# Row-tiled projections and two-bank vector work in a mixed attention and mixture-of-experts kernel

## The chip, the cores and the metric

One core of one Trainium2 chip. The metric is device microseconds (us) for one execution. The kernel before takes 1044.51 us (median of 3 runs, 1044.15 to 1045.33).

Engine names as the profile has them: PE is the matrix engine (PEld its weight loads), DVE the vector engine, ACT the scalar engine, POOL the general engine. PSUM is the memory that the matmuls write (`P` and `ps` in the profile); the kernel uses it as eight banks of 512 fp32 columns. A "512-column matmul" moves 512 columns. The "granted clock" is the share of PE's full clock that the profile records as granted: 1.00 is full speed, "half clock" is 0.5. A "ring" is a set of buffers that are handed out in turn.

## The reference, cut to what matters

```python
def phi(x):                                   # q and k: 8 batches, 8 heads, 576 rows, 64 dims
    proj = einsum('bhsd,df->bhsf', x, w_phi)  # contraction over 64, 128 features
    proj = proj - max(abs(proj), axis=-1)
    return concatenate([exp(proj), exp(-proj)], axis=-1)
kv  = einsum('bhsf,bhsd->bhfd', phi(k), v)
out = einsum('bhsf,bhfd->bhsd', phi(q), kv) / (einsum('bhsf,bhf->bhs', phi(q), z) + 1e-6)
x   = out as (4608, 512)                      # input of the mixture of experts
P   = exp(x @ w_gate - max); 8 rounds of row and column normalisation
y   = sum over 8 experts e of P[:, e] * (relu(x @ w1[e]) @ w2[e])
```

The contraction of the projections runs over 64 only, half of the 128 rows that the profile gives for these matmuls (`128*128`). That is what the change is aimed at.

## The kernel before: the parts that matter

Attention works on 32 pairs of heads (8 batches, 4 pairs). All operations of attention and of the first expert (expert 0, used as filler work for PE) are put into a list, with costs; a Python list scheduler then decides the order of every engine. A string gives the priority of the steps.

```python
order = (   # a: keys, q: queries, r: rest rows, b: kv and numerators, c: transposes, g: gate,
            # u/d: expert 0 up/down.  Cut; 188 steps in all
    "aqraqabbcqabqacbqrbcaqbacuqaqbacqruabgqccucbudbduaqabdqadgrcbucqucabqcauqdua" ...)

ring(ps, [128, 512], FP32, "P1", 8)          # eight PSUM buffers of one bank each
ring(a_t, [128, 2, 4, 128], BF16, f"q{x}", 2)   # rings of two for the tiles of a pair

def scores(x, n):                            # keys (x=1) and query maxima (x=0); n is 1
    for c0 in range(0, 4, 2 * n):
        pp = new(f"P{n}")
        for c in range(2 * n):               # wphi2f: 128 x 256, block-diagonal copies of w_phi
            pe(256, ... mm(pp()[:, 256*c:256*c+256], qkT(x, c0 + c, 1), wphi2f, True, True) ...)
        maxes(512 * n, ...)                  # DVE, one bank
        if x == 1:
            for y, sg in ((0, 1.0), (1, -1.0)):
                exp(512 * n, ...)            # ACT, one bank

def queries():
    mq = scores(0, 1)
    for p0 in range(0, 2, 1):
        pt = new("P1")
        pe(512, ... mm(pt()[:, 0:512], wphi2[:, p0, :], qkT(0, 0, 4), True, True) ...)
        for y, sg in ((0, 1.0), (1, -1.0)):
            exp(512, ...)                    # ACT, one bank

def up(w1, g, hT, fcs, n, r=(), w=()):       # expert 0: four contraction steps of 512 columns
    for f0 in fcs[::n]:
        ph = new(f"P{n}")
        for i in range(n):
            for dc in range(NP):
                pe(512, ... mm(ph()[...], w1()[:, dc, ...], xT[:, dc, ...], dc == 0, dc == NP - 1) ...)
        act(512 * n, ... Relu from ph to hT ...)
```

Two heads lie in the two halves of the partitions. The block-diagonal weight, padded with zeros, projects both at once with the whole array: half of the multiplications are by zero.

## Time and profile before

| stage | span (us) | what runs |
|---|---|---|
| attention mixed with expert 0 | 0 to 219 | all engines; 78 to 209 is its full part |
| leftover expert 0, routing beneath it | 219 to 263 | PE back to back |
| experts 1 to 7 | 263 to 1043 | PE back to back |

The head of the profile's page: busy time of each engine, its share of the span, and its instructions.

```profile
span 1043.5 us, 24529 instructions
PE 1020.4 (98%) x9512; PEld 842.1 (81%) x9512; DVE 823.9 (79%) x1626; ACT 711.1 (68%) x1570; POOL 461.5 (44%) x532
PEclk9999999999999999999999999999999999999999
```

The table of windows for the start and the full part of attention. Columns: window, length, busy us of each engine (number of instructions), then PE's granted clock, DMA share, GB/s.

```profile
core 0: us, PE busy (x) PEld busy (x) DVE busy (x) ACT busy (x) POOL busy (x), PEclk, DMA share, GB/s
0.00:26.00 26.00, 17.36 (x147) 12.63 (x147) 17.09 (x36) 18.26 (x45) 9.59 (x25) 1.00 0.94 250
26.00:52.00 26.00, 21.91 (x252) 14.39 (x252) 24.56 (x60) 24.23 (x63) 21.75 (x40) 1.00 1.01 150
78.00:209.00 131.00, 129.49 (x1426) 83.78 (x1425) 118.38 (x295) 123.00 (x315) 82.91 (x166) 1.00 0.81 133
```

In the full part all three engines look nearly level: PE 99%, ACT 94%, DVE 90%.

The groups of instructions before 220 us (PE) and in 78 to 209 us (DVE, ACT): line, engine, operation, names, shapes and count; then busy us, mean ns of one; then idle time before it and what ended it. One fence for each engine.

```profile
L407 PE MATMUL P<-wphi,qkT 128*128 128x256 bf16 x256 | 39.3, 277 | 1.5 <-DVE wphi L760 0.8 <-DVE xb_r L631 0.3 <-DVE m L399 0.2
L407 PE MATMUL P<-qkT,wphi 128*128 128x512 bf16 x64 | 21.6, 387 | 1.4 <-DVE m_r L399 0.9 <-DVE m L399 0.5
```

```profile
L399 DVE TENSOR_REDUCE m<-P 128x4 f32<-128x512 f32 x81 | 52.6, 681 | 0.5 <-ACT k L403 0.4
```

```profile
L403 ACT ACTIVATE q<-P 128x512 bf16<-128x512 f32 x82 | 46.2, 630 | 3.5 <-PE P L606 2.2 <-PE P L407 1.2
L403 ACT ACTIVATE k<-P 128x512 bf16<-128x512 f32 x84 | 44.3, 629 | 1.6 <-PE P L407 1.5
```

The two PE lines are the work that the change tiles: 256 and 64 matmuls.

Three stretches of PE's timeline (start, duration, engine, line, operation): a group of four projections, the last gate group, and the first matmuls of expert 1.

```profile
178.23 0.60 PE L407 MATMUL P<-wphi,qkT 128*128 128x256 bf16 x4
178.66 0.55 PE L407 MATMUL P<-wgate,xT 128*128 128x8 bf16 x16
...
218.91 0.95 PE L407 MATMUL P<-wgate,xT 128*128 128x8 bf16 x32
...
263.21 0.60 PE L1019 MATMUL P<-xT,w 128*128 128x256 bf16 x4
```

The marked durations overlap (the group of four is marked 0.60 us long, and the next group starts 0.43 us after it), so starts are what to read. The group of four holds PE from 178.23 to 178.66, 0.109 us for 256 columns. The last gate group (the matmuls `x @ w_gate` of the last rows) marks the end of attention.

### The profile page before, as it was taken

What the parts mean: (1) busy time and instruction counts of PE and PEld (TensorE: products, weight loads), DVE (VectorE), ACT (ScalarE), POOL (GpSimd) and SP (SyncE); (2) the same over time, 40 slices, a digit from 0 to 9 for tenths busy, and PEclk for the clock granted to TensorE, in tenths of its full rate; (3) what the DMA queues carried; (4) which work ended last, traced back from release to release, by engine and by line L of the source; (5) the groups of instructions that cost most, each with busy time, mean ns of one, the idle gap of its engine ahead of it and who ended that gap; (6) DMA issues with size and microseconds to landing.
All of it is one profiled execution on the core that took longest, in us unless ns stands there. A gap on an engine that the chain in (4) does not pass through costs nothing.

```text
span 1043.5 us, 24529 instructions
## 1 busy us (share of the span) xinstructions
PE 1020.4 (98%) x9512; PEld 842.1 (81%) x9512; DVE 823.9 (79%) x1626; ACT 711.1 (68%) x1570; POOL 461.5 (44%) x532
## 2 busy tenths in 40 slices
PE   6899999999999999999999999999999999999998
PEld 4566666654788888888888888888888888888886
DVE  6999899998777787778877787778777877787775
ACT  7999999944976666666666666565666666666663
POOL 3876757500233344344444444444444443333442
PEclk9999999999999999999999999999999999999999
DMA  9997987734411152113311441134111611114333
GB/s 250 150 196 132 150 127 136 122 122 120 93 41 41 52 105 60 51 42 82 81 41 42 87 87 51 42 69 95 41 42 50 125 51 42 41 43 131 122 122 122
DMA packets 105237, 93.94 MB, mean 90 GB/s; under 512 B 45344, under 2 KB 80288, under 8 KB 105120
## 3 DMA queue, kind: packets, MB, share of 16 engines
q1 hardware_dynamic: 71840, 68.45, 23.6%
q0 software_dynamic: 33120, 23.86, 16.4%
q8 instruction: 74, 1.21, 0.5%
q14 instruction: 43, 0.35, 0.1%
q10 hardware_dynamic: 160, 0.07, 0.0%
HBM read 94.98 MB, written 14.16 MB: 105 GB/s over the span
## 4 chain that ended last, share of the span: by engine, by line
PE 89%; ACT 5%; DVE 3%; DMA 1%; issue 1%; SPq 0%; POOL 0%; DVEq 0%; ACTq 0%
PE P L1019 70%; PE P L407 16%; ACT acc L1181 2%; DVE m L399 1%; PE P L606 1%; ACT k L403 1%; DMA acc<-in_q_dram 1%; DMA wgate_f<-in_moe_w_gate_dram 1%; ACT V L1171 1%; ACT U L1047 1%; PE P L645 1%; DVE xb L626 0%; ACT q L403 0%; DVE P L618 0%; PE P L484 0%
## 5 line engine op out<-in xcount | busy, mean ns | idle before, releaser
L1174 POOL TENSOR_TENSOR acc<-acc,V 128x512 f32<-128x512 f32 x248 | 316.4, 1283 | 440.4 <-ACT V L1171 437.2
L1051 DVE CUSTOM_DVE_ANT_0 hT<-P,U 128x512 bf16<-128x512 f32 x378 | 255.0, 687 | 107.9 <-ACT U L1047 59.7
L1047 ACT COPY U<-P 128x512 f32<-128x512 f32 x378 | 217.8, 590 | 137.4 <-PE P L1019 130.8
L1171 ACT ACTIVATE V<-P,P 128x256 f32<-128x256 f32 x496 | 206.3, 477 | 123.4 <-PE P L1019 121.6
L1159 DVE SCALAR_TENSOR_TENSOR acc<-P,P,acc 128x256 f32<-128x256 f32 x372 | 160.1, 478 | 73.4 <-PE P L1019 71.7
L1019 PEld LDWEIGHTS <-w 128*128 128x128 bf16 x2016 | 197.3, 98 | 23.7 <-issue 0.6
L1019 PEld LDWEIGHTS <-S 128*128 128x128 bf16 x1984 | 194.1, 98 | 23.2 <-issue 0.6
L1019 PEld LDWEIGHTS <-T 128*128 128x128 bf16 x1512 | 147.9, 98 | 19.1 <-issue 2.0
L1019 PEld LDWEIGHTS <-hT 128*128 128x128 bf16 x1488 | 145.4, 98 | 18.3 <-DVE hT L1051 1.1
L1019 PE MATMUL P<-X,w 128*128 128x256 bf16 x1008 | 154.7, 273 | 0.4 <-ACT U L1047 0.4
L1019 PE MATMUL P<-xT,w 128*128 128x256 bf16 x1008 | 152.0, 273 | 0.0
L1019 PE MATMUL P<-X,T 128*128 128x256 bf16 x1008 | 148.6, 273 | 1.3 <-ACT U L1047 1.2
L1019 PE MATMUL P<-w,hT 128*128 128x256 bf16 x992 | 142.6, 273 | 0.6 <-DVE hT L1051 0.6
L1019 PE MATMUL P<-T,S 128*128 128x256 bf16 x1056 | 136.3, 273 | 0.4 <-ACT V L1171 0.4
L1019 PE MATMUL P<-w,S 128*128 128x256 bf16 x928 | 126.6, 273 | 0.0
L532 POOL TENSOR_TENSOR v<-v_m,em 128x512 bf16<-128x512 f32 x64 | 66.8, 1043 | 70.6 <-ACT em L403 57.5
L399 DVE TENSOR_REDUCE m<-P 128x4 f32<-128x512 f32 x128 | 82.7, 681 | 1.7 <-PE P L407 1.2
L1056 ACT ACTIVATE hT<-P 128x512 bf16<-128x512 f32 x126 | 74.6, 607 | 12.9 <-PE P L1019 12.4
L407 PE MATMUL P<-w,hT 128*128 128x512 bf16 x320 | 80.2, 379 | 0.3
L927 DVE TENSOR_TENSOR S<-hT 128x1024 bf16<-128x1024 bf16 x124 | 80.1, 683 | 0.0
L407 PE MATMUL P<-xT,w 128*128 128x512 bf16 x288 | 76.2, 379 | 1.2 <-ACT kr L403 0.5
L1019 PE MATMUL P<-xT,T 128*128 128x256 bf16 x504 | 76.3, 273 | 0.0
(94 smaller groups left out, 1091.7 us busy)
## 6 DMA issues: line engine op xcount, KB each, us to landing
X<-xd SPq DMA_DIRECT2D x126, 256.0 KB, 2.6
w<-in_moe_w_dram POOLq DMA_DIRECT2D x14, 1024.0 KB, 10.4
v_m<-in_v_dram SPq DMA_DIRECT2D x15, 512.0 KB, 5.1
out_dram<-acc SPq DMA_DIRECT2D x14, 512.0 KB, 3.2
xd<-S SPq DMA_DIRECT2D x18, 256.0 KB, 2.0
qk<-in_k_dram POOLq DMA_DIRECT2D x12, 256.0 KB, 5.5
qk<-in_q_dram POOLq DMA_DIRECT2D x12, 256.0 KB, 6.4
w<-in_moe_w_dram POOLq DMA_DIRECT2D x8, 256.0 KB, 7.5
```

The lines of the kernel that those rows point to most:

```text
L399: dve(el, lambda: nc.vector.tensor_reduce(out=dst(), in_=src(), axis=AX.X, op=ALU.max, apply_absolute_value=True), r, w)
L407: nc.tensor.matmul(out_, lhsT=lhsT, rhs=rhs, start=start, stop=stop)
L532: pool(512, lambda y=y, em=em: nc.gpsimd.tensor_tensor(out=s["v"][y]()[:, :, 0:D], in0=t["v"]()[:, h0:h0 + 2].rearrange("p a (b c) -> p (a ...
L927: lambda: f.tensor_tensor(out=out_(), in0=x(), in1=y(), op=op), r, w, **kw)
L1019: pe(256, lambda i=i, k=k, z=z: nc.tensor.matmul(bank()[:, 256 * i:256 * i + 256], lhsT=lhs(k, i), rhs=rhs(k), start=first and z, stop=k = ...
L1047: act(512, lambda: nc.scalar.copy(out=u[fp][n]().rearrange("p a b -> p (a b)"), in_=x[fp]()), [x[fp]], [u[fp][n]])
L1051: dve(500, lambda: nc.vector._custom_dve(ADD_SAT, out=out_(fp, i, j), in0=bank[fp]().rearrange("p (a b) -> p a b", a=2), in1=u[fp][n](), s ...
L1056: act(512, lambda: nc.scalar.activation(out=out_(fp, i, j), in_=x[fp]().rearrange("p (a b) -> p a b", a=2), func=ACT.Relu, bias=0.0, scale ...
L1159: dve(330, lambda n=n, ts=ts: nc.vector.scalar_tensor_tensor(out=acc[g][:, ts, 256 * j:256 * j + 256], in0=bank()[:, 256 * n:256 * n + 256 ...
L1171: act(390, lambda n=n: nc.scalar.activation(out=u()[:, n, :], in_=bank()[:, 256 * n:256 * n + 256], func=ACT.Copy, bias=0.0, scale=P[:, 4 ...
L1174: pool(670, lambda: nc.gpsimd.tensor_tensor(out=acc[g][:, 2 * i:2 * i + 2, 256 * j:256 * j + 256], in0=acc[g][:, 2 * i:2 * i + 2, 256 * j: ...
L1181: act(512, lambda ts=ts: nc.scalar.activation(out=acc[g][:, ts, :], in_=acc[g][:, ts, :], func=ACT.Copy, bias=0.0, scale=P[:, 4 * g + ts, ...
```

## The change

Its intent: (1) each zero-padded projection becomes two matmuls of 64 rows, meant to run on the upper and the lower half of the array at the same time, each writing its own PSUM bank; (2) query maxima, query exps and numerators read two neighbouring banks in one instruction, so ACT and DVE issue fewer; (3) more buffers for the tiles of a pair, placed inside the second weight tiles, which are idle during attention; (4) finer steps in the order string (query maxima and query features apart, kv and numerators apart). PSUM becomes one tile whose banks are handed out one or two at a time.

```diff
-        def scores(x, n):
-            for c0 in range(0, 4, 2 * n):
-                pp = new(f"P{n}")
-                for c in range(2 * n):
-                    pe(256, lambda c=c, c0=c0, pp=pp: mm(
-                        pp()[:, 256 * c:256 * c + 256], qkT(x, c0 + c, 1), wphi2f,
+    def mm2(banks, stat, mov, n):
+        for c in range(n):
+            for x in range(2):
+                rows = slice(64 * x, 64 * x + 64)
+                w = 512 // n
+                nc.tensor.matmul(banks[x]()[:, w * c:w * c + w],
+                                 lhsT=stat(c)[rows], rhs=mov(c)[rows], start=True, stop=True)
+    def pe2(cols, two_, stat, mov, n, r, takes=()):
+        plan.op("PE", n * max(cols / 2400.0 + 0.0025, 0.06) + 0.08, 0.32,
+                lambda: mm2(two_[1], stat, mov, n), r, two_[0], takes)
+        def scores(x):
+            merged = (1, 0)[x]                 # query maxima take two neighbouring banks
+            pp = two(merged)
+            pe2(128, pp, lambda c: qkT(x, c, 1), lambda c: wphi, 4, ...)
+        def queries():
+            pt = two(1)
+            pe2(512, pt, lambda c: wphi, lambda c: qkT(0, 0, 4), 1, ...)
@@ cut: numerators in one two-bank tile; rings @@
-    ring(ps, [128, 512], FP32, "P1", 8)
+    R["P1"], R["P2"] = Banks(ps, banks, 1), Banks(ps, banks, 2)
-        ring(a_t, [128, 2, 4, 128], BF16, f"q{x}", 2)
+        ring(a_t, [128, 2, 4, 128], BF16, f"q{x}", 2, 1)     # 1 more, inside the weight tile
@@ cut: the order string, now with p (query features) and n (numerators) as steps of their own @@
```

A "group" below is one call of `mm2`: eight tiled matmuls of 128 columns, or two of 512. There are 104 of them.

## The prediction

> **What bounds it now.** The windows view splits the span in three. (1) Attention mixed with expert 0, 0–219 us: in 78–209 us PE is marked busy 129.5 of 131 us, ACT 123.0, DVE 118.4; in 0–78 us PE 63.6, ACT 67.5, DVE 66.9 of 78. (2) Leftover expert-0 matmuls, 219–263 us, back to back on PE; routing (P written at 257.6) hides under them. (3) Experts 1–7, 263–1043 us, matmuls at a pitch of 0.109 us per 256 columns. The chain of waits is 89% PE. The change touches mainly stage 1[...]. With PE pitches from the timeline (0.216 us per 512 columns, 0.03 per 65) I sum about 189 us of PE work before the last gate, which ends at 219.7. ACT, 190.5 of 209 us, looks tightest.
>
> **What changes, with durations from the trace.**
> - ACT: 128 query exps of 512 become 64 of 1024; 32 kr exps of 256 become 16 of 512: 80 instructions fewer. 512 columns have a pitch of 0.49 us, about 0.06 above streaming. About −5 us.
> - DVE: five instructions fewer per pair (a maximum, a multiply, a reciprocal, two xb), 160 in all, each with a fixed part of about 0.07 us (a 512-wide maximum repeats every 0.60 us). About −11 us.
> - PE: projections become pairs of 64-row matmuls. [...] With perfect concurrency 189 becomes about 169 us. The changed instruction order has 172 mode switches; at an estimated 0.05–0.1 us each (part of the 0.17 us that a short matmul lasts beyond its pitch) 9–17 us come back. Net −3 to −11 us.
> - Deeper pair rings and finer steps let ACT and DVE wait less; of ACT's 19 idle us before 209, about 8 are the DMA-fed start and stay.
> - Expert 1's weights load after attention. A megabyte lands in 10.4 us (DMA issues), routing takes 38 us: hidden.
> - Banks are picked most recently freed first. In the expert stage the PE work between a bank's last write and its reuse falls from a median of 4.8 us (minimum 2.0) to 2.7 (mostly at least 1.3), by the instruction order. An eviction takes 0.6–0.7 us, so I expect 0–4 us of small PE waits.
>
> **On the critical path.** Attention's end moves with the tightest engine: ACT, about 185 us of work plus 14 idle, then the tail. I expect the last gate at about 209 instead of 220 us (−10), everything after it shifted, +1 for bank reuse.
>
> **Predicted: 1035 us**, 8 in 10 within 1026–1044. Faster by over 2%: 5%; within 2%: 92%; slower: 3%. More than 2% would need attention to end before 199 us, with some 185 us of ACT work in it.
>
> **What would show each step.** 64 query exps of 1024 at about 1.05 us; DVE busy before the last gate about 10 us lower; paired matmuls starting within nanoseconds of one another, and a gap around each group; last gate near 209 us; expert 1 starting near 253 us, its stage (780 us) unchanged within 4; no wait for expert 1's weights.
>
> **What would make it wrong.** Row tiles that do not overlap, or switches of 0.15 us and more: PE becomes tightest and the gain vanishes. An order that front-loads attention and then starves PE. Bank reuse that stalls every one of the 63 groups: +5 to +10 us. Upwards: packing that removes nearly all ACT idle.

The sum was 1044.5 us, 10 less by an earlier last gate and 1 more for bank reuse, given as 1035. In PE's term the 20 us of streaming saved (189 to 169) stand on an assumption, "with perfect concurrency", and the 9 to 17 us that come back on the estimate from the 0.17 us. The item on ACT and that on DVE do not say how streaming was told from the fixed part. Back-to-back starts before 220 us (medians) do: ACT's are 0.263 and 0.477 us apart for 256 and 512 columns in the kernel before, and 0.905 for 1024 in the changed one, so one instruction for two saves 0.049 us; DVE's maxima are 0.598 us apart for 512 (before) and 1.131 for 1024 (after), so it saves 0.065 us.

## The result, and the profile after

The changed kernel takes 1044.51 us (median of 4 runs, 1044.21 to 1044.92); the kernel before took 1044.92 us (1044.15 to 1046.4) in the same rounds. The ratio is 0.9994, with a 95% interval of 0.998 to 1.0008: the same time. It was predicted at 1035 us, and 1044.51 is outside the range of 1026 to 1044. A ratio here is the mean time of one kernel's fast runs over that of the other's of the same rounds, so it is not quite the ratio of the medians quoted beside it.

The same views of the changed kernel. First the head of the page:

```profile
span 1042.4 us, 24890 instructions
PE 1014.3 (97%) x9819; PEld 832.6 (80%) x9864; DVE 817.4 (78%) x1466; ACT 709.1 (68%) x1490; POOL 463.3 (44%) x532
PEclk9899999999999999999999999999999999999999
```

DVE has 160 instructions fewer and ACT 80, as foreseen. PE shows 9819 matmuls but 9864 weight loads: 45 matmul records are missing from this trace, so its idle time can't be taken from matmul starts without care.

The windows:

```profile
0.00:26.00 26.00, 18.41 (x155) 14.08 (x157) 15.53 (x27) 17.85 (x40) 13.17 (x32) 0.93 0.98 255
26.00:52.00 26.00, 20.25 (x299) 15.01 (x298) 24.02 (x42) 22.83 (x49) 17.88 (x35) 0.80 0.96 142
78.00:209.00 131.00, 126.76 (x1644) 73.71 (x1670) 113.61 (x193) 120.83 (x267) 80.77 (x161) 1.00 0.74 119
```

DVE is 4.8 us less busy and ACT 2.2 us in the full part. PE's 126.76 lacks the missing records. PE's granted clock is 0.93 and 0.80 in the first two windows, where it was 1.00. The clock records show two stretches at half clock, at 21.7 us for 3.4 us and at 38.7 us for 10.2 us. Sixteen 65-column matmuls in a row are marked 1.09 us long in the second of them, at 46.38 us, and 0.68 us before it, at 36.48 us. In the 3.4 us before each stretch PE streamed for 1.1 and 1.2 us, and its longest marked wait was 1.40 and 0.94 us. In the profiled execution of the untiled kernel of the same order (e1, below) there was no such stretch in the first 50 us. What sets the half clock off was not shown.

The groups:

```profile
L500 PE MATMUL ps<-wphi,qkT 64*128 64x128 bf16 x512 | 26.2, 230 | 4.4 <-DVE m L476 1.0 <-DVE xb L719 1.0 <-DVE wx L476 0.7
L500 PE MATMUL ps<-qkT,wphi 64*128 64x512 bf16 x64 | 13.2, 412 | 1.7 <-DVE m L476 1.1
```

```profile
L476 DVE TENSOR_REDUCE m<-ps 128x4 f32<-128x512 f32 x28 | 18.9, 682 | 1.6 <-PE ps L500 1.4
L476 DVE TENSOR_REDUCE m<-ps 128x8 f32<-128x1024 f32 x15 | 18.3, 1218 | 2.3 <-PE ps L500 2.3
```

```profile
L480 ACT ACTIVATE k<-ps 128x512 bf16<-128x512 f32 x56 | 29.5, 610 | 1.0 <-PE ps L500 0.8
L480 ACT ACTIVATE q<-ps 128x1024 bf16<-128x1024 f32 x28 | 27.5, 1030 | 1.5 <-PE ps L500 1.1
```

(Buffers that lie inside the weight tile appear as `wx` in lines of their own, so the counts here are not whole.) Busy time of the tiled projections fell from 39.3 to 26.2 us and from 21.6 to 13.2 us. One exp over 1024 columns takes 1.03 us where two over 512 took 1.26.

PE's timeline around two tiled groups, the last gate group, and expert 1:

```profile
188.78 0.40 PE L500 MATMUL ps<-wphi,qkT 64*128 64x128 bf16 x8
189.11 0.60 PE L484 MATMUL ps<-w,hT 128*128 128x512 bf16 x2
189.64 0.40 PE L500 MATMUL ps<-wphi,qkT 64*128 64x128 bf16 x8
189.97 0.60 PE L484 MATMUL ps<-w,hT 128*128 128x512 bf16 x2
...
218.28 0.95 PE L484 MATMUL ps<-wgate,xT 128*128 128x8 bf16 x32
...
261.95 0.93 PE L1100 MATMUL ps<-xT,wx 128*128 128x256 bf16 x7
```

From 189.11 to 189.64 there are two matmuls of 0.216 us and 0.10 us of nothing (0.096 us, the median after a 512-column matmul that a tiled one follows). From 189.64 to 189.97 there are four pairs at 0.056 us, 0.22 us together, and 0.11 us of nothing. So a lone tiled group costs 0.10 + 0.33 = 0.43 us of PE, and before it cost 0.43 us. Tiling halved the streaming and the two mode switches gave it back, to within 0.01 us. The last gate group starts at 218.28 us, 0.6 us earlier than before; it was predicted ten earlier. The stage of experts 1 to 7 has its old length (780.5 us, before 780.3).

How PE spends 78 to 220 us: the matmuls that start in this window, counted by shape, times the pitches seen in the trace (0.216 us per 512 columns, 0.109 per 256, 0.056 per 128, 0.030 per 65); a tiled pair counts once; idle is the rest. Other ways to count the short matmuls move a figure by about 1 us. The third column is e15 below, which has 64 tiled groups in this window and a trace without missing records.

| us of PE in 78 to 220 | before | new order, untiled (e1) | new order, tiled (e15) |
|---|---|---|---|
| streaming | 136.6 | 137.6 | 125.1 |
| mode switches | 0 | 0 | 11.1 |
| idle | 5.4 | 4.4 | 5.8 |

Before, PE streams for 136.6 of 142 us. It is 96% full. That is the number which the prediction should have had.

The rows of a column add up to 142 whatever happens, so progress has to be read as well. The changed kernel, e1 and e15 issue the same PE work in the same order. Laid beside e1, the trace of the changed kernel shows where 44 of its 45 missing records belong: all are 512-column matmuls, 30 of them in this window. With these, it has 124.3 us of streaming, about 11.5 of switches and 6 of idle time. PE work done since the start, each step at its untiled cost, in one execution each:

| us of untiled PE work done by | 20 us | 26 us | 52 us | 78 us | 220 us |
|---|---|---|---|---|---|
| new order, untiled (e1) | 8.7 | 13.5 | 30.3 | 53.5 | 190.9 |
| changed kernel | 8.6 | 11.3 | 27.4 | 51.1 | 190.0 |
| e15 (first 40 groups untiled) | 8.7 | 12.8 | 29.4 | 52.6 | 191.8 |

From 78 to 220 us the changed kernel does 138.9 us of this work and e1 137.4: in the full part, tiling does gain, 1.5 us. It enters this part 2.4 us behind e1, and 2.2 of these were lost between 20 and 26 us.

### The profile page after: what moved, and what is told of

Read it like the earlier page. It is cut to its first block, busy times and chain, and to the rows that moved or that the text cites. A ratio compares the mean times of both kernels' runs of the same rounds, so it can differ in the third digit from the quotient of the medians.

```text
span 1042.4 us, 24890 instructions
## 1 busy us (share of the span) xinstructions
PE 1014.3 (97%) x9819; PEld 832.6 (80%) x9864; DVE 817.4 (78%) x1466; ACT 709.1 (68%) x1490; POOL 463.3 (44%) x532
## 3 DMA queue, kind: packets, MB, share of 16 engines
q8 instruction: 77, 1.26, 0.5%
## 4 chain that ended last, share of the span: by engine, by line
PE 88%; DVE 5%; ACT 3%; DMA 2%; issue 1%; POOL 1%; SPq 0%; DVEq 0%; POOLq 0%; ACTq 0%
PE ps L1100 71%; PE ps L484 12%; PE ps L500 2%; DMA acc<-in_q_dram 1%; PE ps L705 1%; ACT acc L1262 1%; DVE m L476 1%; DMA qkT<-qk 1%; DVE S L1008 1%; PE ps L728 1%; DVE xb L719 0%; DVE acc L1240 0%; ACT wx L480 0%; PE ps L580 0%; ACT U L1128 0%
## 5 line engine op out<-in xcount | busy, mean ns | idle before, releaser
L1132 DVE CUSTOM_DVE_ANT_0 hT<-ps,U 128x512 bf16<-128x512 f32 x378 | 254.9, 687 | 106.1 <-ACT U L1128 52.4
L1128 ACT COPY U<-ps 128x512 f32<-128x512 f32 x378 | 218.0, 589 | 143.5 <-PE ps L1100 136.2
L1252 ACT ACTIVATE V<-ps,P 128x256 f32<-128x256 f32 x496 | 206.0, 476 | 117.9 <-PE ps L1100 107.9
L1240 DVE SCALAR_TENSOR_TENSOR acc<-ps,P,acc 128x256 f32<-128x256 f32 x372 | 159.5, 478 | 70.4 <-PE ps L1100 68.7
L1100 PE MATMUL ps<-X,T 128*128 128x256 bf16 x1008 | 148.6, 273 | 0.5 <-ACT U L1128 0.5
L1100 PE MATMUL ps<-T,S 128*128 128x256 bf16 x1056 | 136.3, 273 | 0.0
L1100 PEld LDWEIGHTS <-wx 128*128 128x128 bf16 x1152 | 112.7, 98 | 14.7 <-issue 1.4
L1100 PEld LDWEIGHTS <-w 128*128 128x128 bf16 x864 | 84.5, 98 | 11.0 <-issue 1.2
L1100 PE MATMUL ps<-X,wx 128*128 128x256 bf16 x576 | 88.5, 273 | 0.9 <-ACT U L1128 0.9
L1100 PE MATMUL ps<-xT,wx 128*128 128x256 bf16 x576 | 87.1, 273 | 0.0
```

The costliest lines, as they stand in the source:

```text
L1100: pe(256, lambda i=i, k=k, z=z: nc.tensor.matmul(bank()[:, 256 * i:256 * i + 256], lhsT=lhs(k, i), rhs=rhs(k), start=first and z, stop=k = ...
L1128: act(512, lambda: nc.scalar.copy(out=u[fp][n]().rearrange("p a b -> p (a b)"), in_=x[fp]()), [x[fp]], [u[fp][n]])
L1132: dve(500, lambda: nc.vector._custom_dve(ADD_SAT, out=out_(fp, i, j), in0=bank[fp]().rearrange("p (a b) -> p a b", a=2), in1=u[fp][n](), s ...
L1240: dve(330, lambda n=n, ts=ts: nc.vector.scalar_tensor_tensor(out=acc[g][:, ts, 256 * j:256 * j + 256], in0=bank()[:, 256 * n:256 * n + 256 ...
L1252: act(390, lambda n=n: nc.scalar.activation(out=u()[:, n, :], in_=bank()[:, 256 * n:256 * n + 256], func=ACT.Copy, bias=0.0, scale=P[:, 4 ...
```

## The experiments

Theory A (formed after the result): PE's own time bounded attention before and after; switches give back what tiling saves; ACT and DVE savings lie off the critical path. Rivals: B, ACT bounds attention as predicted and something new holds it back; C, the half clock in the first 50 us eats the gain; D, the new order or the deeper rings cost something that hides a gain. Eighteen kernels ran.

### e1_full: the new order without tiling

```diff
-                rows = slice(64 * x, 64 * x + 64)
-                     lhsT=stat(c)[rows], rhs=mov(c)[rows], ...
+                     lhsT=padded(stat(c), x), rhs=padded(mov(c), x), ...   # zero-padded w_phi
```

> Undoes the row tiling alone: every projection uses all 128 rows, with zero-padded weights, in the same instruction order, so there is no mode switch. Theory A (PE bounds attention[...]): both costs vanish with the saving, the clock is 1.00 throughout and the time stays within 5 us of 1044 (1040 to 1049). Rival B (row tiling gains some 20 us of PE time that is not on the critical path because ACT or inputs bound attention): PE has room, also within 5 us, but PE idle before the last gate shrinks by some 20 us. Rival C (row tiling gained on the critical path and something else lost it): 10 us slower or more.

In the text above, "both costs" are those that theory A counted against about 23 us of streaming saved: 172 switches at the measured 0.10 us, about 17 us, and an estimated 7 us, half of the 13.7 us at half clock.

Measured: 1044.22 us, ratio 0.9984 (0.997 to 0.9999), no switch, granted clock 0.999, last gate group at 217.52 us. Untiled, the changed kernel takes the same time. So the tiling as a whole is worth nothing here, and everything else in the change is worth about 1.7 us (0.1 to 3.1 by the interval).

### e2_warm and e7_warm2: keeping the clock up by repeating work

```diff
-        for c in range(n):
+        for c in list(range(n)) * rep:     # e2: the first 26 groups x3; e7: groups 12 to 17 x4
```

> The changed kernel, but each of the first 26 projection groups (up to about 50 us) is issued three times into the same bank, so that PE is kept busy; results unchanged. Theory A: the two half-clock stretches (21.7-25.1 and 38.7-49.0 us) shrink or vanish and the last gate comes 2 to 6 us earlier (time 1038 to 1042). Rival (the clock does not matter there, since DVE, ACT and the input DMAs bound the first 78 us): clock back to 1.00, time 1043 to 1047.

> A narrower test of the clock than e2_warm: only projection groups 12 to 17 in the order of execution (about 29 to 39 us) are issued four times, 3.6 us of PE work where PE idles about 4 us. If the half-clock stretch at 38.7-49.0 us costs time, it is gone and the time falls by 2 to 5 us; if DVE, ACT and inputs set the pace up to 50 us, the clock rises and the time stays within 1 us of the changed kernel (1044.5).

Measured: e2 1045.21 us, ratio 1.0002 (0.9985 to 1.0018), one half-clock stretch of 3.4 us left, last gate at 221.82. e7 1045.98 us, ratio 1.0011 (0.9997 to 1.0026), the long stretch shortened from 10.2 to 6.8 us. Neither met the gain that the clock theory expected, but both add PE work of their own, so they leave C open. e14 and e15 try it without added work.

### e3_pen8 and e4_inputs: two attempts to re-plan, both misses

```diff
# e3: the scheduler charges 0.8 us for leaving tiled mode and so groups tiled work: 106 switches
+        if o.eng == "PE" and self.mode and not o.tiled:
+            free = free + 0.8
# e4: a third qkT buffer in place of the third q0/q1
-    ring(a_t, [128, 2, 8, 128], BF16, "qkT", 2)
+    ring(a_t, [128, 2, 8, 128], BF16, "qkT", 2, 1)
-        ring(a_t, [128, 2, 4, 128], BF16, f"q{x}", 2, 1)
+        ring(a_t, [128, 2, 4, 128], BF16, f"q{x}", 2)
```

> The changed kernel with a scheduler that prefers a further row-tiled group while PE is in that mode: 106 switches in place of 172, the same instructions. Theory A: [...]time 1036 to 1041 unless the new order makes waits of its own. Rival B (PE is not what bounds attention): no change, 1042 to 1047.

Theory A in the text of e3: 66 switches fewer at the measured 0.10 us would save 6 to 7 us of PE time.

> The changed kernel with a third buffer for the transposed q and k (in the place of the third query-feature buffer). Rival D (attention is starved by the transposes of its inputs, of which one shows a 9.4 us wait at 72-81 us in the chain of waits): that wait shrinks and the time falls by 4 us or more. Theory A: no gain beyond 2 us.

Measured: e3 1090.15 us (ratio 1.0433), e4 1087.84 us (ratio 1.0402); the last gate comes at 263.0 and 260.6 us. Both expectations missed. In e3 PE is busy for only 41.8 of the 52 us from 78 on. The order string fits one set of costs and ring sizes; any change of either makes another schedule, which here starves PE. Neither run says anything on switches or on qkT by itself.

### e5_moresw: more switches

```diff
+            if c == 2:     # a full-array matmul of one column in the middle of a group of four
+                nc.tensor.matmul(banks[0]()[:, 384:385], lhsT=stat(3), rhs=mov(3)[:, 0:1],
+                                 start=True, stop=True)
```

> The changed kernel with one one-column full-array matmul in the middle of each four-chunk projection group (its column is overwritten afterwards): 316 mode switches in place of 172, nothing else. Theory A (PE bounds attention and a switch costs 0.1 us of it): 144 more switches cost about 14 us, time 1055 to 1061. Rival B (switches fall into time in which PE would wait anyway): less than 5 us, 1044 to 1049.

Measured: 1054.9 us, ratio 1.0093 (1.0073 to 1.0112), correct, last gate at 229.93. 144 switches more, with the 72 one-column matmuls that make them, cost 10.4 us (1054.9 - 1044.5), 0.07 us each. That is a little below the expected range; perhaps some fall where PE waits anyway. The time that PE loses between a matmul of one mode and the next of the other, summed over 78 to 220 us, rose from 11.8 to 20.0 us. Switches are on the critical path.

### e8_split: the two-bank instructions taken apart

```diff
-                    exp(512 * n, lambda ...: s["T"][y]()[:, i:i + n] ..., buf, sg, ...)
+                    def both(...):
+                        for k in range(2):       # one ACT instruction per bank
+                            nc.scalar.activation(... in_=buf()[:, 512 * k:512 * k + 512] ...)
# the same for DVE's maxima, multiplies, reciprocals and quotients
```

> The changed kernel with every two-bank DVE and ACT instruction split back into one per bank (64 exps, 32 maxima, 32 multiplies, 32 reciprocals, 64 products more), in the same order. Theory A (DVE and ACT do not bound attention after about 80 us): within 3 us, 1043 to 1048. Rival (my prediction's step: ACT bounds attention, DVE near it): the 5 us of ACT and 11 us of DVE come back as 5 to 11 us, 1049 to 1056.

Measured: 1046.64 us, ratio 1.0019 (1.0002 to 1.0036). DVE's busy time in 78 to 209 us is back at 118.05 us and ACT's at 122.08, and the time is some 2 us above the changed kernel's, with intervals that just overlap. So the savings on ACT and DVE, estimated in the prediction at 5 and 11 us, are worth about 2.

### e9_merge: 30 switches fewer

After scheduling, 15 tiled groups are moved forward to the previous tiled group where data and banks allow it (142 switches).

```diff
-        done = self.schedule()
+        done = self.gather(self.schedule())   # cut: moves a tiled group forward past untiled PE work
```

> The changed kernel with 15 row-tiled groups moved forward to stand next to an earlier one, after scheduling: 142 switches in place of 172, all else in the same order. Theory A: 3 us less, 1040 to 1043, if the moved groups do not wait for their inputs. Rival B: no change, 1043.5 to 1046.

Measured: 1044.65 us, ratio 1.0 (0.9985 to 1.0015). The expected 3 us did not come. Switching in 78 to 220 us fell from 11.8 to 9.3 us, and idle time rose by 2.9 us (both traces lack 45 matmul records, so the difference stands). A group moved forward may wait in its new place for its inputs or banks. That this is what happened is the reading of the sums; no single wait was traced.

### e10_oldorder and e11_oldfull: the old order in the changed kernel

```diff
-        "aprqbaqaqpnabbqbnraqppbaqmcpbanpmnqmncnamqaqbrappnqbnmbamppacnbmqbmpqmpcacan" ...
+        "aqpraqpabnbncqpabnqpacbnqprbncaqpbnacuqpaqpbnacqpruabngqpccucbnudbnduaqpabnd" ...
# e11: the same, with the untiled projections of e1
```

> The changed kernel with the order of steps of the kernel before (q becomes q and p, b becomes b and n); tiled, deeper rings, two-bank instructions; 178 mode switches instead of 172. If the finer order was only the means of feeding the tiled pairs and any good order does (theory: TensorE work sets the time), it comes within 4 us of 1044.5. If the new order carries a gain of its own that hides the cost of switching, this run is slower by 5 to 30 us.

> The same old order with full-array projections padded with zeros: no tiling, no mode switch, only two-bank instructions and deeper rings remain. If TensorE streaming was the bound before and ACT and DVE were close behind, it lands near the full-array run of the new order, 1043 to 1045 us. If the new order matters by itself, it is slower than that run by more than 3 us.

Measured: e10 1069.75 us, ratio 1.0237 (1.0221 to 1.0252); e11 1068.23 us, ratio 1.0224 (1.0208 to 1.0239). Tiled or not, the old order costs 24 to 25 us in the changed kernel (1069.75 against 1044.51 tiled, 1068.23 against 1044.22 untiled), although it gave 1044.9 in the kernel before. So the new order is not a gain of its own over the kernel before: it is what the two-bank claims and the other new costs of the schedule need to get back to even. Which of the new pieces the old order suits so badly was not separated.

### e12_light and e13_lightb: PE work taken out

```diff
 # e12: the changed kernel; e13: the kernel before. Wrong result on purpose.
                         xT[:, dc, g * 512:(g + 1) * 512], dc == 0, dc == NP - 1)
+                        if not (light and dc == 2) else None,
-        up(W[0][0], g, hts[g], (2 * part, 2 * part + 1), 1, w=["up0"])
+        up(..., light=6 <= 4 * g + part < 24)
```

> The changed kernel with 36 matmuls of expert 0 (one of four contraction steps in 18 of the up steps, nearly all after 78 us) left out, so 36 x 0.216 = 7.8 us less TensorE work at unchanged order; wrong result on purpose. If TensorE is the bound of the changed kernel after 78 us, it ends 6 to 8 us earlier, about 1037.5. If another limit stands right behind it (order and latency, ACT at 121 of 131 us), it gains under 4 us, 1040.5 or more.

> The kernel before with the same 36 matmuls left out (wrong result on purpose). TensorE is 97% streaming from 78 us there: if it is the bound, the time falls by 6 to 8 us to about 1037.5. If ACT is (what the prediction said), it falls by under 3 us.

Measured: e12 1038.63 us, ratio 0.9942 (0.9927 to 0.9957): 5.4 us (by the ratios) to 5.9 us (by the medians) below the changed kernel, of 7.8, just under the 6 to 8 that were expected; the last gate at 214.18. The changed kernel is bound mainly by PE. e13 1041.8 us, ratio 0.9973 (0.9956 to 0.9989): 2.8 of 7.8 us by the ratio (0.0027 x 1044.9), the last gate at 215.46. It fell between the two expectations: PE counts before the change too, but another limit stands some 3 us behind it.

### e14_hyb24, e15_hyb40, e16_runs: tiling in places

```diff
+        n_mm2[0] += 1
+        full = n_mm2[0] <= 24        # e15: <= 40; e16: every group that stands alone among untiled work
+        def part(v, x):
+            if full:
+                return wphi2[:, x, :] if v is wphi else v      # zero-padded, whole array
+            return v[64 * x:64 * x + 64]
```

> The changed kernel with the first 24 projection groups (all that run before 52 us) on the full array with zero-padded features, the other 80 tiled; 142 switches, same order. If the half clock and the switches of the first 50 us cost time, the half-clock stretches vanish and it ends 2 to 5 us before the changed kernel, 1040 to 1042.5. If they are hidden in the start-up's waits, 1044 to 1045.

> The same with the first 40 groups (till about 80 us) on the full array; 114 switches. The start-up should then keep pace with the full-array run (59 fills of expert 0 done by 78 us against 41), and the tiled rest save what single groups leave: 1039 to 1042.5 if start-up counts, 1044 to 1045 if not.

> Only the 34 groups that stand in stretches of two or three in the order of the changed kernel are tiled, the 70 lone ones use the full array; 32 switches. If a lone tiled group costs what an untiled one does, 1043.5 to 1044.5, like the full-array run and the changed kernel. If switching costs more than the trace's 0.10 us[...], it is faster than both by 2 us or more.

Measured: e14 1044.68 us, ratio 0.9992 (0.9976 to 1.0009). e15 1043.35 us, ratio 0.9988 (0.9973 to 1.0004). e16 1045.98 us, ratio 1.0007 (0.9995 to 1.0019). In the profiled execution of e15 the half clock is gone:

```profile
0.00:26.00 26.00, 16.79 (x171) 13.24 (x172) 17.70 (x32) 18.13 (x42) 13.34 (x32) 1.00 0.99 256
26.00:52.00 26.00, 19.73 (x312) 15.56 (x310) 24.65 (x44) 24.35 (x51) 19.13 (x37) 1.00 1.02 150
78.00:209.00 131.00, 128.76 (x1685) 74.87 (x1684) 113.04 (x193) 121.49 (x268) 80.02 (x160) 1.00 0.71 116
```

The granted clock, the third figure from the end of a line, is 1.00 in the first two windows, where the changed kernel had 0.93 and 0.80, and the time is the same within the interval, whose lower end (0.9973) allows some 3 us. So C falls as the cause of a gain of 10 us being missed. It does not fall as a cost of 1 to 3 us. The result of each run lists the granted clock of every execution. Over e14 and e15 together, the six executions at 0.999 or more (in the profiled one of e15 this means no half clock but at the very end) took 1041.6 to 1043.8 us (mean 1042.3), and the six at 0.998 or less took 1043.8 to 1047.5 (mean 1045.8). The profiled execution of e14 was one of the latter, with one stretch at half clock, at 21.5 us for 3.4 us. Up to 50 us e14 and e15 are the same program; both had done 8.7 us of PE work at 20 us, and at 26 us it was 11.3 in e14 and 12.8 in e15. The stretch of 10.2 us at 38.7 us in the changed kernel cost less: from 26 to 52 us it did 16.1 us of work, e15 16.6 and e1 16.8. This sorting was done after the fact. It shows that the half clock goes with lost time, not that it causes all of it: a late input may bring both.

e16 tiles only the 34 groups that stand in stretches of two or three (32 switches) and leaves the 70 lone groups untiled. It takes the time of the changed kernel with its 172 switches, and of e1 with none, within 0.3%: a lone tiled group gains nothing. Its median came out above the 1043.5 to 1044.5 that was expected, with the kernel before at 1044.98 in the same rounds; four of its five executions had a granted clock of 0.995 or 0.996, and the fifth, at 0.999, took 1044.44. These three runs spread more than others (1041.6 to 1047.5), and none of them is shown to beat either kernel.

### e17_fulllight: the untiled new order with less PE work

The edits of e1 and e12 together.

> The full-array run of the new order with the 36 expert 0 matmuls left out (wrong result on purpose), 7.8 us less TensorE work. If the two-bank instructions and deeper rings took away the limit that stood behind TensorE in the kernel before, it gains 6 to 8 us on the full-array run's 1044.2: 1036.5 to 1038.5. If it was the tiling, it gains about 3 us: 1041 or more.

Its output is wrong, which doesn't matter for the time. Measured: 1042.87 us (1038.88 to 1045.17), ratio 0.9971 (0.9952 to 0.999). That is about 1.3 us below e1 by the ratios, but the six runs spread over 6 us. The two executions at a granted clock of 0.999 or more took 1038.9 and 1039.5, some 5 us below e1; the four at 0.997 or 0.998 took 1042.5 to 1045.2. So the mean does not look as if the two-bank instructions alone removed the limit that stands behind PE before the change, and the two clean executions look as if they did; this stays open.

### e18_actlight and e19_bothlight: ACT work taken out of the kernel before

```diff
-                out=ht()[:, f0 % 4:f0 % 4 + n, :] ..., in_=ph()[:, 0:512 * n], func=ACT.Relu, ...
+                out=ht()[:, f0 % 4:f0 % 4 + n, 0:few] ..., in_=ph()[:, 0:few * n], func=ACT.Relu, ...
                     # few = 128 for batches 2 to 5; their down matmuls read columns 0:128 throughout
# e19: with the PE cut of e13 as well
```

> The kernel before with 32 of ACT's Relu evictions of expert 0 cut from 512 to 128 columns (batches 2 to 5; their down matmuls read the first 128 columns throughout, so TensorE work is unchanged; wrong result on purpose). An estimate from ACT's 128x512 at 0.64 us and 128x256 at 0.41 us: about 0.3 us each, 10 us less ACT work. If ACT was the bound (the prediction's step), 6 to 10 us faster, 1035 to 1039. If TensorE was, under 3 us, 1042 or more.

> The same ACT cut together with the 36 matmuls left out (7.8 us of TensorE). If ACT is the limit that stood behind TensorE, the gain is near the sum's limit, 6 to 8 us or more, 1037 to 1039. If the second limit is the order and its latencies (PSUM banks, waits of one step for the last), it stays near the 3 us of the TensorE cut alone, 1041 to 1042.

ACT's Relu evictions of expert 0 in e18, before 260 us:

```profile
L699 ACT ACTIVATE hT<-P 128x512 bf16<-128x512 f32 x40 | 23.8, 614 | 18.6 <-PE P L407 18.5
L699 ACT ACTIVATE hT<-P 128x128 bf16<-128x128 f32 x32 | 8.7, 299 | 0.2 <-PE P L407 0.2
```

Its window of the full part of attention:

```profile
78.00:209.00 131.00, 128.09 (x1409) 83.83 (x1431) 118.36 (x296) 115.36 (x315) 82.89 (x166) 1.00 0.79 131
```

Thirty-two evictions fell from 0.61 to 0.30 us, 10 us in all (32 x 0.315). ACT's busy time in the window went from 123.00 to 115.36 us, 88% of it. Measured: e18 1044.86 us, ratio 1.0 (0.9987 to 1.0013). Ten microseconds of ACT work less moved nothing: B falls. (Its result stayed within the tolerance, against what the expectation said.) e19: 1041.5 us, ratio 0.9973 (0.996 to 0.9987): the very ratio of e13. Its output is wrong, which doesn't matter for the time. With ACT lightened, the PE cut gains no more than without. ACT is not the second limit either.

## Why the prediction was wrong, point by point

- "ACT, 190.5 of 209 us, looks tightest" and "Attention's end moves with the tightest engine: ACT": this is the step that failed. e18 took 10 us of ACT work out of the kernel before, and the time did not move (ratio 1.0). PE was the tighter one: 7.8 us of its work taken out gave 2.8 us in the kernel before (e13) and 5.4 to 5.9 in the changed one (e12). The predicted gain of 10 us rested on ACT setting the end. ACT was 94% busy in the full part and still had slack. The prediction compared three busy shares; PE's own was 99% in the same line, and by starts and pitches it streamed 136.6 of 142 us. Its sum of "about 189 us of PE work" set the thinly filled first 78 us (about 51 us of streaming) against the whole and so made PE look looser than it was where it mattered.
- ACT -5 us and DVE -11 us: the instruction counts fell as predicted (80 and 160). Taking the two-bank instructions apart again (e8) costs about 2 us. They are mostly off the critical path.
- "Net -3 to -11 us" on PE: the sign of the terms was right. Concurrency was an assumption when it was written; the trace of the changed kernel shows it, about four in five tiled pairs start 3 to 6 ns apart. It also shows 0.10 us lost on each side of a tiled stretch. The estimate of 0.05 to 0.1 us a switch holds at its upper end, 172 x 0.10 = 17 us, against 23 us of streaming saved (72 x 0.224 + 32 x 0.216): net -6 us of PE work, inside the range. So the size of this term was right, and even so it did not shorten the run. What the prediction did not ask is how tiled groups lie in the order: of 86 tiled stretches 70 hold one group, and a lone group of eight costs 0.43 us tiled and untiled. In the full part of e15 (tables above) tiling saves 14.2 us of streaming (half of 28.4) and 11.1 us go to switches; of the 3 us left, 1.4 become waiting and 1.7 more work done than in e1. In the changed kernel the start loses what the full part gains. Over the whole run nothing is left, as e1, e16 and the changed kernel show.
- "Switches of 0.15 us and more: PE becomes tightest" was named as a way to be wrong. The switches are cheaper than that, and PE was the tightest before the change too, with another limit some 3 us behind it (e13).
- "Deeper pair rings and finer steps let ACT and DVE wait less": not gained. The old order in the changed kernel is 24 to 25 us slower, so the new order is needed, and it brings the kernel back to where it was. The rings were not tested alone; e4, which moved one buffer, became 4% slower by its new schedule.
- Bank reuse "0 to 4 us": nothing. The expert stage keeps its length, 780.5 against 780.3 us. Expert 1's weights hidden: right.
- Half clock: not foreseen. Some 13.7 us of the start run at half clock. With the first 40 groups untiled (e15) the executions without it took about 2 us less than the changed kernel and those with it did not, so it, or what brings it, costs a part of the missing gain. It is no explanation of 10 us.

What stays open: the limit that stands about 3 us behind PE in the kernel before (e13). It is not ACT (e19). DVE (118.4 of 131 us busy in the full part), or the order of the instructions and its latencies are left; no run separated them. Nor is it settled why the changed kernel follows its PE work for the most part (e12) while the untiled new order does so in two executions only (e17), nor what share of the lost 2.4 us of the start is due to the half clock.

## What to carry to other kernels

Before a change that lightens several nearly level engines, find out which one bounds: take some work out of one engine alone, at unchanged order, and time it; busy shares of 94% and 99% look alike in a profile and were worth 0 and 3 us here for 10 and 7.8 us of work. Row tiling is to be counted by stretches here, not by matmuls: a tiled stretch paid 0.10 us at each end, and a lone group of eight cost 0.43 us tiled and untiled. So count the mode switches in the final instruction order, and compare a whole lone group, switches included, with the untiled one. This follows from the sums of the traces; no run showed a gain in time from fewer switches or from tiling the longer stretches alone (e9, e16). An order string that was tuned for one set of costs and buffers is part of the kernel: with another set it must be tuned again before anything is concluded.
